# Sharing a TensorE transpose between the 64 tail columns of two x row tiles, in the head of a two-layer squared-ReLU kernel

## The chip, the cores and the metric

The kernel runs on one core of one Trainium2 chip. The metric is the device time of one execution in microseconds (us). The profile's *span* is measured from the first instruction to the last and is some 1.7 to 1.9 us shorter than the device time. Engines are named as the profile names them: PE is TensorE's matmuls, PEld its weight loads, DVE is VectorE, ACT is ScalarE, POOL is GpSimd, and SPq and ACTq are the queues on which DMA transfers are issued.

## The reference

```python
B, S, D, F = 1, 2048, 576, 4608            # all arrays bf16
h = einsum("bsd,df->bsf", x, w1) + b1
r = where(h > 0, h, 0)
out = einsum("bsf,fd->bsd", r * r, w2) + b2
```

The contraction length D = 576 is four and a half times the 128 rows of TensorE. The kernel cuts D into nine chunks of 64 columns, and most of the first layer runs as pairs of 64-row matmuls, one on each half of the array. Both halves need x transposed, with D on the partitions, and each half needs chunks that the other half holds. That is what the copies below are for.

## The kernel before

For the first block of 512 rows, x is loaded as four row tiles of 128 rows and transposed on TensorE. Four transposes of 128 columns cover columns 0 to 511. The last 64 columns need a fifth, which takes the last 128 columns, half of them for the second time.

```python
load_x(nc.sync, 0); load_x(nc.scalar, 1); load_x(nc.sync, 2); load_x(nc.scalar, 3)
for k in range(NK):                                  # NK = 4: chunks of w1n, 128 KB each
    load_w1n(nc.sync if k % 2 == 0 else nc.scalar, k, k + 1)
# ... cut ...
PLACE = [(0, 0), (0, 1), (1, 0), (1, 1), (0, 2)]
T_ORDER = [0, 1, NK, 2, 3]

def x_transpose(j):                                  # five transposes of one row tile
    h, q = divmod(j, 2)
    for k in T_ORDER:
        bank, slot = PLACE[k]
        c0 = k * P if k < NK else D - P
        transpose(tb[h][bank][:, slot, q*P:(q+1)*P], xs[:, j, c0:c0+P], ident)

def x_copies(h):                                     # PSUM -> xT0, for 256 rows
    for k in (0, 1): vector.tensor_copy(xT0[:, O+k, hc], tb[h][0][:, k, :])
    scalar.copy(xT0[:, O+2:O+4, hc], tb[h][1][:, 0:2, :])
    vector.tensor_copy(xT0[:, E3, hc], tb[h][0][:, 2, :])

def dup_windows(sb):                                 # shifted copies between the two halves
    vector.tensor_copy(xT[0:H, SPC:SPC+4, :], xT[H:P, E3:E3+4, :])
    vector.tensor_copy(xT[H:P, SPC:SPC+4, :], xT[0:H, O:O+4, :])

# the head ("keep" pins the order of the program):
for j in range(2): x_transpose(j)
x_copies(0)
for j in range(2, 4): x_transpose(j)
x_copies(1); dup_windows(0)
for k in range(NK): part(0, k)      # 4 matmuls of width 256 each: w1n chunk k, row half 0
part(1, 0); make_b1T()
for k in range(1, NK): part(1, k)
# then the row pair (w1n8, 64-row matmuls), their evictions, and the main loop over w1_h
```

Of the kernel before, what the change touches and what calls it, by code (L numbers as in the profile page):

```python
# [11 lines left out]
BF16 = mybir.dt.bfloat16  # L12
# [5 lines left out]
def kernel(  # L18
# [9 lines left out]
    nc = tc.nc  # L28
    keep = tc.keep_in_program_order
    P = 128  # L30
    H = 64
    x2 = x.flatten_outer_dims()
    out2 = out.flatten_outer_dims()
    S, D = x2.shape
# [3 lines left out]
    NK = NC // 2  # L38
# [6 lines left out]
    RT = SB // P  # L45
# [3 lines left out]
    const = ctx.enter_context(tc.tile_pool(name="const", bufs=1))  # L49
# [6 lines left out]
    ps_h = ctx.enter_context(tc.tile_pool(name="ps_h", bufs=4, space=PSUM))  # L56
# [8 lines left out]
    xs = const.tile([P, RT, D], BF16, name="x_sb")  # L65
# [12 lines left out]
    def load_w1n8(eng, h):  # L78
        keep(eng.dma_start(out=w1n8[h * H:(h + 1) * H, :], in_=w1[NK * P:D, 0:GW]))
# [14 lines left out]
    ident = const.tile([P, P], BF16, name="ident")  # L94
# [3 lines left out]
    keep(nc.scalar.dma_start(out=b1_rows[0:NFT, :], in_=b1.rearrange("(ft p) -> ft p", p=P)))  # L98
    for h in range(2):
        load_w1n8(nc.sync, h)  # L100

    E3, O, SPC, E = 0, 1, 5, 6
    LO_W = [O, O + 1, O + 2, O + 3, E, E + 1, E + 2, E3, SPC]
# [9 lines left out]
    def dup_windows(sb):  # L113
        xT = xT_blk[sb]
        keep(nc.vector.tensor_copy(out=xT[0:H, SPC:SPC + 4, :], in_=xT[H:P, E3:E3 + 4, :]))  # L115
        keep(nc.vector.tensor_copy(out=xT[H:P, SPC:SPC + 4, :], in_=xT[0:H, O:O + 4, :]))  # L116
# [18 lines left out]
    xT0 = xT_blk[0]  # L135
    HS = SB // 2
    tb = [[ps_h.tile([P, 4, HS], BF16, name="tb", tag="ph") for _ in range(2)] for _ in range(2)]
    PLACE = [(0, 0), (0, 1), (1, 0), (1, 1), (0, 2)]
    T_ORDER = [0, 1, NK, 2, 3]

    def x_transpose(j):
        h, q = divmod(j, 2)
        for k in T_ORDER:
            bank, slot = PLACE[k]
            c0 = k * P if k < NK else D - P
            keep(nc.tensor.transpose(tb[h][bank][:, slot, q * P:(q + 1) * P], xs[:, j, c0:c0 + P], ident[:]))

    def x_copies(h):
        hc = slice(h * HS, (h + 1) * HS)
        for k in (0, 1):  # L150
            keep(nc.vector.tensor_copy(out=xT0[:, O + k, hc], in_=tb[h][0][:, k, :]))
        keep(nc.scalar.copy(out=xT0[:, O + 2:O + 4, hc], in_=tb[h][1][:, 0:2, :]))  # L152
        keep(nc.vector.tensor_copy(out=xT0[:, E3, hc], in_=tb[h][0][:, 2, :]))

    b1T = const.tile([P, NFT], FP32, name="b1T")

    def make_b1T():
        b1T_ps = ps_h.tile([P, P], BF16, name="b1T_ps", tag="ph")
        keep(nc.tensor.transpose(b1T_ps[:], b1_rows[:], ident[:]))  # L159
        keep(nc.vector.tensor_copy(out=b1T[:], in_=b1T_ps[:, 0:NFT]))  # L160
# [6 lines left out]
    def evac_h(sb, bank, ft):  # L167
        r = rpool.tile([P, SB], BF16, name="r", tag="r")
        keep(nc.scalar.activation(out=r[:], in_=bank[:], func=ACT.Relu, bias=b1T[:, ft:ft + 1], scale=1.0))  # L169
        keep(nc.vector.tensor_tensor(out=hTs[sb][:, ft, :], in0=r[:], in1=r[:], op=ALU.mult))  # L170
# [17 lines left out]
    def a_full(sb, order):  # L188
        xT = xT_blk[sb]
        banks = []  # L190
        for g in range(G):
            pool, tag = (ps_o, "po") if g < 2 or order == "k_outer" else (ps_h, "ph")
            banks.append(pool.tile([P, SB], FP32, name="pn", tag=tag))

        def pair(i, start, stop):
            keep(nc.tensor.matmul(banks[2 * i][:], lhsT=w1n8[0:H, 2 * i * P:(2 * i + 1) * P], rhs=xT[0:H, SPC, :],  # L196
                             start=start, stop=stop, skip_group_check=order == "k_outer"))
            keep(nc.tensor.matmul(banks[2 * i + 1][:], lhsT=w1n8[H:P, (2 * i + 1) * P:(2 * i + 2) * P], rhs=xT[H:P, E3, :],  # L198
                             start=start, stop=stop, skip_group_check=order == "k_outer"))

        def full(g, k, start, stop):
            keep(nc.tensor.matmul(banks[g][:], lhsT=w1n[:, k, g * P:(g + 1) * P], rhs=xT[:, O + k, :],  # L202
                             start=start, stop=stop))

        if order == "rows_first":
            for i in (1, 0):
                pair(i, True, False)
            for g in (2, 3, 0, 1):
                for k in range(NK):
                    full(g, k, False, k == NK - 1)  # L210
                evac_h(sb, banks[g], g)
        else:
            if order == "k_outer":
                def part(h, k):
                    hc = slice(h * HS, (h + 1) * HS)
                    for g in range(G):
                        keep(nc.tensor.matmul(banks[g][:, hc], lhsT=w1n[:, k, g * P:(g + 1) * P],  # L217
                                              rhs=xT[:, O + k, hc], start=(h == 0 and k == 0), stop=False,
                                              skip_group_check=True))

                for j in range(2):
                    x_transpose(j)
                x_copies(0)
                for j in range(2, RT):
                    x_transpose(j)
                x_copies(1)
                dup_windows(0)
                for k in range(NK):
                    part(0, k)
                part(1, 0)  # L230
                make_b1T()
                for k in range(1, NK):
                    part(1, k)
            else:
                for g in (2, 3, 0, 1):
                    for k in range(NK):
                        full(g, k, k == 0, False)
            for i in (1, 0):
                pair(i, False, True)
                evac_h(sb, banks[2 * i], 2 * i)  # L240
                evac_h(sb, banks[2 * i + 1], 2 * i + 1)
# [42 lines left out]
    b2_col = const.tile([P, 1], BF16, name="b2_col")  # L284
    keep(nc.sync.dma_start(out=b2_col[:], in_=b2[DM:D].rearrange("(d o) -> d o", o=1)))
    b2T = const.tile([P, 1], FP32, name="b2T")
    nc.gpsimd.tensor_copy(out=b2T[:], in_=b2_col[:])
    keep(nc.sync.dma_start(out=b2_bc[:], in_=b2.partition_broadcast(P)))
    for c in range(2):
        load_w2(c)  # L290
# [1 line left out]

    alloc_hT(0)
    a_full(0, "k_outer")
    a_rows(0, 12, 1)
    alloc_hT(1)
    load_xT(3)
    a_rows(1)
    a_full(1, "rows_first")
    phase_t(0, hTs[0])  # L300
    phase_t(1, hTs[1])
    phase_b(0, hTs[0], dups=(2, 3))
    phase_b(1, hTs[1])
    alloc_hT(2)
    a_full(2, "g_outer")
    a_rows(2)
    alloc_hT(3)
# [36 lines left out]
```

## Time and profile before

| | before |
|---|---|
| device time, median | 290.67 us (three runs), 290.95 us with three more of the comparison |
| profiled span | 288.7 us |
| TensorE busy | 284.6 us, 99% of the span |
| first transposes / first chunk matmul / row pair / main loop | 3.76 / 5.41 / 9.06 / 9.50 us |

Everything that the change touches lies ahead of 9.5 us, and behind it TensorE runs without a break. The prediction shows TensorE's own lines of this stretch. What VectorE does in it, in order of time, is this (start, busy length, engine, line, operation, shapes, count, and the idle time before with its releaser):

```profile
4.42 0.49 DVE L151 COPY xTw<-tb 128x256 bf16<-128x256 bf16 x2 [3.49 <-PE tb L146]
6.44 0.69 DVE L115 COPY xTw<-xTw 64x2048 bf16<-64x2048 bf16 x1 [0.54 <-ACT xTw L152]
7.16 0.69 DVE L116 COPY xTw<-xTw 64x2048 bf16<-64x2048 bf16 x1
7.88 0.20 DVE L160 CAST b1T<-b1T_ps 128x36 f32<-128x36 bf16 x1
```

The shifted copies and the bias are finished at 8.08, and the row pair needs the copies at 9.06: VectorE is not late.

### The profile page before, as it was taken

To read this page: it belongs to the slowest core of one execution; us is meant where nothing else is said; L and a number is where in the kernel's file an instruction comes from. 1 tells how busy PE (TensorE), PEld (TensorE's weight loads), DVE (VectorE), ACT (ScalarE), POOL (GpSimd) and SP (SyncE) were. 2 spreads that over 40 slices of the span, in tenths; PEclk is the share of its full clock that TensorE was granted. 3 is DMA by queue.
4 is the path that set the end of the run, shared out by engine and by line. 5 is a ranking of instruction groups with operands and counts; after the bars stand their busy time and mean duration, and the time that the engine had idled before them with its cause. 6 is when DMAs were issued, how large, how long until landed. Compare 5 with 4: busy or idle time off the path is not lost.

```text
span 288.7 us, 4690 instructions
## 1 busy us (share of the span) xinstructions
PE 284.6 (99%) x2027; PEld 138.9 (48%) x2032; DVE 78.6 (27%) x177; ACT 96.5 (33%) x152; POOL 0.9 (0%) x7
## 2 busy tenths in 40 slices
PE   8999999999999999999999999999999999999996
PEld 5544444444444555555544444444444455555555
DVE  3444544444500200000025444444440001100001
ACT  3666666666500000000027666666670000000000
POOL 0000000000000000000000000000000000000000
PEclk9999999999999999999999999999999999999999
DMA  6999999600001100000000000000000110000000
GB/s 198 236 244 197 265 388 246 94 0 2 0 18 36 37 16 18 16 16 18 16 16 2 1 2 0 2 0 2 0 2 0 36 39 16 16 16 19 32 17 18
DMA packets 31573, 16.59 MB, mean 57 GB/s; under 512 B 15552, under 2 KB 31552, under 8 KB 31552
## 3 DMA queue, kind: packets, MB, share of 16 engines
q1 hardware_dynamic: 30928, 15.72, 22.3%
q10 hardware_dynamic: 624, 0.57, 0.7%
q8 instruction: 16, 0.26, 0.4%
q14 instruction: 5, 0.04, 0.0%
HBM read 11.43 MB, written 2.36 MB: 48 GB/s over the span
## 4 chain that ended last, share of the span: by engine, by line
PE 97%; DMA 1%; SPq 0%; issue 0%; DVE 0%
PE ph L181 42%; PE po L272 38%; PE pt L253 11%; PE pn L202 4%; DMA w1n<-in_w_dram 1%; PE pn L217 1%; PE ph L183 1%; PE pn L196 1%; SPq L72 0%; DVE o_sb L274 0%; PE b1T_ps L159 0%; PE pn L198 0%
## 5 line engine op out<-in xcount | busy, mean ns | idle before, releaser
L181 PE MATMUL ph<-xTw,w_h 64*128 64x512 bf16 x576 | 124.6, 376 | 0.0
L183 PE MATMUL ph<-xTw,w_h 64*128 64x512 bf16 x576 | 124.6, 376 | 0.0
L272 PE MATMUL po<-w_sb,hT 128*128 128x448 bf16 (+2 forms) x612 | 109.4, 341 | 0.0
L169 ACT ACTIVATE r<-ph,b1T 128x512 bf16<-128x512 f32 x128 | 81.1, 685 | 41.6 <-PE ph L183 41.6
L181 PEld LDWEIGHTS <-w_h 64*128 64x128 bf16 x576 | 54.1, 94 | 68.3
L272 PEld LDWEIGHTS <-hT 128*128 128x128 bf16 x612 | 58.5, 98 | 51.0
L170 DVE TENSOR_TENSOR hT<-r 128x512 bf16<-128x512 bf16 x144 | 61.2, 426 | 76.9 <-ACT r L169 76.9
L183 PEld LDWEIGHTS <-w_h 64*128 64x128 bf16 x576 | 54.1, 94 | 0.0
L274 DVE TENSOR_TENSOR o_sb<-po,b_bc 128x448 bf16<-128x448 f32 (+2 forms) x17 | 10.2, 597 | 125.8 <-PE po L272 125.8
L253 PE MATMUL pt<-hT,w_sb 128*128 128x512 bf16 x142 | 31.3, 379 | 0.1
L169 ACT ACTIVATE r<-pn,b1T 128x512 bf16<-128x512 f32 x16 | 10.3, 688 | 62.0 <-PE pn L198 60.6
L253 PEld LDWEIGHTS <-w_sb 128*128 128x128 bf16 x144 | 14.1, 98 | 17.0
L256 ACT ACTIVATE oT<-pt,b2T 128x512 bf16<-128x512 f32 x4 | 2.7, 687 | 28.3 <-PE pt L253 28.3
L202 PE MATMUL pn<-xTw,w1n 128*128 128x512 bf16 x45 | 10.4, 379 | 0.4 <-issue 0.3
L202 PEld LDWEIGHTS <-w1n 128*128 128x128 bf16 x48 | 4.5, 98 | 6.0 <-issue 0.8
L217 PE MATMUL pn<-xTw,w1n 128*128 128x256 bf16 x32 | 3.7, 273 | 0.1
L63 PE MATMUL wps<-const-bfloat16-1.0 128*128 128x512 bf16 (+1 forms) x7 | 2.9, 597 | 0.8 <-PEq L328 0.8
L217 PEld LDWEIGHTS <-w1n 128*128 128x128 bf16 x32 | 3.0, 98 | 0.6 <-DMA w1n<-in_w_dram 0.3
L115 DVE COPY xTw<-xTw 64x2048 bf16<-64x2048 bf16 x4 | 2.8, 690 | 0.6 <-ACT xTw L152 0.5
L116 DVE COPY xTw<-xTw 64x2048 bf16<-64x2048 bf16 x4 | 2.8, 688 | 0.1
L196 PE MATMUL pn<-xTw,w1n 64*128 64x512 bf16 x8 | 2.4, 379 | 0.0
L198 PE MATMUL pn<-xTw,w1n 64*128 64x512 bf16 x8 | 2.4, 379 | 0.0
(21 smaller groups left out, 10.5 us busy)
## 6 DMA issues: line engine op xcount, KB each, us to landing
w_sb<-in_w_dram SPq DMA_DIRECT2D x2, 2592.0 KB, 15.2
w_h<-in_w_dram SPq DMA_DIRECT2D x14, 288.0 KB, 6.6
out_dram<-o_sb SPq DMA_DIRECT2D x15, 112.0 KB, 1.7
w_h<-in_w_dram SPq DMA_DIRECT2D x4, 144.0 KB, 3.2
out_dram<-ot SPq DMA_DIRECT2D x4, 128.0 KB, 2.0
x_sb<-in_x_dram ACTq DMA_DIRECT2D x2, 144.0 KB, 3.0
x_sb<-in_x_dram SPq DMA_DIRECT2D x2, 144.0 KB, 3.0
w1n<-in_w_dram ACTq DMA_DIRECT2D x2, 128.0 KB, 3.6
```

The lines of the kernel that those rows point to most:

```text
L63: keep(nc.tensor.matmul(wps[:, 0:n], lhsT=ones[:, 0:P], rhs=ones[:, 0:n], start=True, stop=True))
L115: keep(nc.vector.tensor_copy(out=xT[0:H, SPC:SPC + 4, :], in_=xT[H:P, E3:E3 + 4, :]))
L169: keep(nc.scalar.activation(out=r[:], in_=bank[:], func=ACT.Relu, bias=b1T[:, ft:ft + 1], scale=1.0))
L170: keep(nc.vector.tensor_tensor(out=hTs[sb][:, ft, :], in0=r[:], in1=r[:], op=ALU.mult))
L181: keep(nc.tensor.matmul(bx[:], lhsT=w1_h[0:H, LO_C[i], jc], rhs=xT[0:H, LO_W[i], :], start=(i == 0), stop=(i == NC - 1)))
L183: keep(nc.tensor.matmul(by[:], lhsT=w1_h[H:P, UP_C[i], jc], rhs=xT[H:P, UP_W[i], :], start=(i == 0), stop=(i == NC - 1)))
L196: keep(nc.tensor.matmul(banks[2 * i][:], lhsT=w1n8[0:H, 2 * i * P:(2 * i + 1) * P], rhs=xT[0:H, SPC, :], start=start, stop=stop, skip_grou ...
L202: keep(nc.tensor.matmul(banks[g][:], lhsT=w1n[:, k, g * P:(g + 1) * P], rhs=xT[:, O + k, :], start=start, stop=stop))
L217: keep(nc.tensor.matmul(banks[g][:, hc], lhsT=w1n[:, k, g * P:(g + 1) * P], rhs=xT[:, O + k, hc], start=(h == 0 and k == 0), stop=False, s ...
L253: keep(nc.tensor.matmul(pt[:], lhsT=w2_sb[:, ft, DM:D], rhs=hT[:, ft, :], start=(i == 0), stop=(i == NFT - 1)))
L272: keep(nc.tensor.matmul(po[:, 0:d1 - d0], lhsT=hT[:, ft, jj * P:(jj + 1) * P], rhs=w2_sb[:, ft, d0:d1], start=(i == 0), stop=(i == NFT - 1)))
L274: keep(nc.vector.tensor_tensor(out=o_sb[:, d0:d1], in0=po[:, 0:d1 - d0], in1=b2_bc[:, d0:d1], op=ALU.add))
```

## The change

The intent is a shorter head. Each row tile gets four transposes instead of five. The 64 tail columns of two row tiles are first put side by side by GpSimd (`xs8`), so that one transpose serves both, and these two transposes stand behind chunk 1 of the first half instead of ahead of all matmuls. The copies from PSUM are ordered bank by bank, with VectorE taking the first half alone. One of the shifted copies of block 0 goes to ScalarE.

```diff
+    xs8 = const.tile([P, RT, H], BF16, name="xs8")
+    for h in range(2):
+        keep(nc.gpsimd.tensor_copy(out=xs8[:, 2 * h:2 * h + 2, :], in_=xs[:, 2 * h:2 * h + 2, NK * P:D]))
...
     def x_transpose(j):
-        for k in T_ORDER:                      # five, see above
+        for bank in range(2):
+            for k in range(2 * bank, 2 * bank + 2):
+                transpose(tb[h][bank][:, k % 2, q*P:(q+1)*P], xs[:, j, k*P:(k+1)*P], ident)
+            for k in range(2 * bank, 2 * bank + 2) if q == 1 else ():
+                copy = nc.scalar.copy if h == 1 and bank == 1 else nc.vector.tensor_copy
+                copy(xT0[:, O + k, hc], tb[h][bank][:, k % 2, :])
+    def dup_windows_first():
+        scalar.copy(xT0[0:H, E:E + 3, :], xT0[H:P, O:O + 3, :])
+    def transpose_tails():
+        for h in range(2):
+            transpose(tl[:, h, :], xs8[:, 2*h:2*h+2, :], ident)
+        for q in range(2): vector.tensor_copy(x8[H:P, E3, :, q, :], tl[q*H:(q+1)*H, 0:2, :])
+        for q in range(2): vector.tensor_copy(x8[0:H, SPC, :, q, :], tl[q*H:(q+1)*H, 0:2, :])
+        vector.tensor_copy(xT0[H:P, SPC:SPC + 4, :], xT0[0:H, O:O + 4, :])
+        vector.tensor_copy(xT0[0:H, E3, :], xT0[H:P, O + 3, :])
...
-                (transposes, x_copies, dup_windows(0), part(0, 0..3), part(1, 0), make_b1T, part(1, 1..3))
+                for j in range(RT): x_transpose(j)
+                dup_windows_first()
+                part(0, 0); part(0, 1)
+                transpose_tails()
+                part(0, 2); part(0, 3)
+                for k in range(NK):
+                    part(1, k)
+                    if k == 1: make_b1T()
```

(Wrappers are dropped from some lines. One tiny copy of `b2` is also pinned in the program order.)

More of the change, by code (lines that the diff above doesn't have):

```diff
@@ L137 @@
     tb = [[ps_h.tile([P, 4, HS], BF16, name="tb", tag="ph") for _ in range(2)] for _ in range(2)]
-    PLACE = [(0, 0), (0, 1), (1, 0), (1, 1), (0, 2)]
-    T_ORDER = [0, 1, NK, 2, 3]
     def x_transpose(j):
         h, q = divmod(j, 2)
-        for k in T_ORDER:
-            bank, slot = PLACE[k]
-            c0 = k * P if k < NK else D - P
-            keep(nc.tensor.transpose(tb[h][bank][:, slot, q * P:(q + 1) * P], xs[:, j, c0:c0 + P], ident[:]))
-    def x_copies(h):
-        hc = slice(h * HS, (h + 1) * HS)
-        for k in (0, 1):
-            keep(nc.vector.tensor_copy(out=xT0[:, O + k, hc], in_=tb[h][0][:, k, :]))
-        keep(nc.scalar.copy(out=xT0[:, O + 2:O + 4, hc], in_=tb[h][1][:, 0:2, :]))
-        keep(nc.vector.tensor_copy(out=xT0[:, E3, hc], in_=tb[h][0][:, 2, :]))
-    b1T = const.tile([P, NFT], FP32, name="b1T")
+        hc = slice(h * HS, (h + 1) * HS)
+        for bank in range(2):
+            for k in range(2 * bank, 2 * bank + 2):
+                keep(nc.tensor.transpose(tb[h][bank][:, k % 2, q * P:(q + 1) * P], xs[:, j, k * P:(k + 1) * P], ident[:]))
+            for k in range(2 * bank, 2 * bank + 2) if q == 1 else ():
+                copy = nc.scalar.copy if h == 1 and bank == 1 else nc.vector.tensor_copy
+                keep(copy(out=xT0[:, O + k, hc], in_=tb[h][bank][:, k % 2, :]))
+    b1T = const.tile([P, NFT], FP32, name="b1T")
+    def dup_windows_first():
+        keep(nc.scalar.copy(out=xT0[0:H, E:E + 3, :], in_=xT0[H:P, O:O + 3, :]))
+    def transpose_tails():
+        tl = ps_h.tile([P, 2, P], BF16, name="tl", tag="ph")
+        for h in range(2):
+            keep(nc.tensor.transpose(tl[:, h, :], xs8[:, 2 * h:2 * h + 2, :], ident[:]))
+        x8 = xT0.rearrange("p c (h q t) -> p c h q t", h=2, q=2)
+        for q in range(2):
+            keep(nc.vector.tensor_copy(out=x8[H:P, E3, :, q, :], in_=tl[q * H:(q + 1) * H, 0:2, :]))
+        for q in range(2):
+            keep(nc.vector.tensor_copy(out=x8[0:H, SPC, :, q, :], in_=tl[q * H:(q + 1) * H, 0:2, :]))
+        keep(nc.vector.tensor_copy(out=xT0[H:P, SPC:SPC + 4, :], in_=xT0[0:H, O:O + 4, :]))
+        keep(nc.vector.tensor_copy(out=xT0[0:H, E3, :], in_=xT0[H:P, O + 3, :]))
     def make_b1T():
@@ L219, in part @@
                                               skip_group_check=True))
-                for j in range(2):
+                for j in range(RT):
                     x_transpose(j)
-                x_copies(0)
-                for j in range(2, RT):
-                    x_transpose(j)
-                x_copies(1)
-                dup_windows(0)
+                dup_windows_first()
+                part(0, 0)
+                part(0, 1)
+                transpose_tails()
+                part(0, 2)
+                part(0, 3)
                 for k in range(NK):
-                    part(0, k)
-                part(1, 0)
-                make_b1T()
-                for k in range(1, NK):
                     part(1, k)
+                    if k == 1:
+                        make_b1T()
             else:
@@ L286 @@
     b2T = const.tile([P, 1], FP32, name="b2T")
-    nc.gpsimd.tensor_copy(out=b2T[:], in_=b2_col[:])
+    keep(nc.gpsimd.tensor_copy(out=b2T[:], in_=b2_col[:]))
     keep(nc.sync.dma_start(out=b2_bc[:], in_=b2.partition_broadcast(P)))
```

## The prediction

> **What bounds the kernel now.** I read the page first (busy shares, then the chain of waits that ended last), then the chain over the first 10 us, and then the timeline of that stretch engine by engine, because the diff touches nothing that runs after about 10 us except one tiny GpSimd copy.
>
> ```profile
> PE 284.6 (99%) x2027; PEld 138.9 (48%) x2032; DVE 78.6 (27%) x177; ACT 96.5 (33%) x152; POOL 0.9 (0%) x7
> PE 97%; DMA 1%; SPq 0%; issue 0%; DVE 0%
> ```
>
> The first line gives busy time per engine in a span of 288.7 us; the second is the share of the chain that ended last. TensorE holds 97% of that chain. So only two things can change the time: the moment at which TensorE starts on work that it then never leaves, and the number of instructions it executes after that moment. The chain over the first 10 us (start, length, what) shows where that moment is:
>
> ```profile
> 0.73 0.40 SPq L72
> 1.20 0.44 SPq L72
> 1.68 3.68 DMA w1n<-in_w_dram
> 5.36 0.05 issue
> 5.41 2.36 PE pn L217 x20
> 7.76 0.06 PE b1T_ps L159
> 7.82 1.31 PE pn L217 x12
> 9.13 0.32 PE pn L196
> ```
>
> The reader is to see that no transpose of x is in it. The path goes through two issues of x loads on the SyncE queue, the load of the first chunk of w1n (3.68 us, landing at 5.36), and then TensorE from 5.41 without a hole: 20 matmuls of L217, the bias transpose, 12 more, the row pair of L196 and L198, and the main loop. Before 5.41 TensorE waits three times, and the timeline of its weight loads says for what:
>
> ```profile
> 3.76 0.56 PEld L146 LDWEIGHTS <-x_sb 128*128 128x128 bf16 x10 [0.75 <-DMA x_sb<-in_x_dram]
> 4.55 0.56 PEld L146 LDWEIGHTS <-x_sb 128*128 128x128 bf16 x10 [0.23 <-DMA x_sb<-in_x_dram]
> 5.40 2.08 PEld L217 LDWEIGHTS <-w1n 128*128 128x128 bf16 x20 [0.29 <-DMA w1n<-in_w_dram]
> ```
>
> Columns are start, busy length, engine, line, instruction, count, and in brackets the idle time before it with its releaser. All 20 transposes of the kernel before lie between 3.76 and 5.11, in two lots of ten, each lot behind an x load; afterwards TensorE idles 0.29 us for w1n. The transposes have slack of 0.29 us.
>
> **What the Trainium skill says.** (1) "TensorE: Matmul & The Clock Gate", Back-to-back issue gap, gives 134 cycles for a moving width of 128 and 262 for 256, which at its 2.4 GHz are 56 ns and 109 ns. The trace agrees: 20 matmuls of width 256 with a duration of 0.273 us took 2.36 us, so their spacing is (2.36 - 0.27)/19 = 0.110 us, and ten transposes kept the weight load busy 0.56 us, 0.056 us each. (2) "VectorE: DVE Perf Modes", perf-mode tier table: a bf16 copy of 2048 elements from SBUF takes 693 ns in the 4x mode, anything from PSUM is capped at 2x. The window copies of L115 and L116 measure 690 ns, so they agree; the copies from PSUM take 0.286 us for 256 elements, two of them in 0.49 us, so one each 0.20 us. (3) "GPSIMD Engine Reference", 3.1, puts elementwise work at 1.8 cycles per element at best; at its 1.2 GHz that is an estimate of 0.19 us for 128 elements. The trace has a GpSimd operation on 128x128 (the second step of the identity) at 0.294 us, and I use 0.3 us. (4) "Advanced Engine Details and Errata", Mode Summary, says that VectorE's second SBUF port is shared with GpSimd, and that they block each other. No row of the kernel before shows such a collision, as GpSimd has nothing to do after 1.3 us there.
>
> **The change part by part.**
>
> *Removed on TensorE:* each of four row tiles had five transposes, one of which (the last 128 columns) was mostly columns already transposed. Now there are four per tile: 20 becomes 16, less 4 x 0.056 = 0.22 us. All four were in front of 5.41, beside a load. The second lot would end about 2 x 0.056 = 0.11 us sooner, at about 5.00, and TensorE would then wait some 0.40 us instead of 0.29 for the same w1n chunk. Gain on the path: nothing, as long as w1n is last.
>
> *Added on TensorE:* two transposes of the tails, between chunks 1 and 2 of the first half. That is after 5.41, on the path: + 2 x 0.056 = +0.11 us. The bias transpose moves from after 20 matmuls to after 24, but costs its 0.06 us in both. The matmuls themselves, 32 of width 256, the pairs and everything later are the same in count and order.
>
> *Copies per bank:* the order is changed so that the first half's chunks 2 and 3 are copied by VectorE instead of ScalarE. Six VectorE copies at 0.20 us pitch, four of them from about 4.45 and two behind the last tile at about 5.0, should be done at about 5.7. The second matmul chunk of the first half starts at 5.41 + 4 x 0.11 = 5.85, chunk 2 at 5.41 + 8 x 0.11 + 0.11 = 6.40: ample. ScalarE has two copies of 256 elements instead of two of 512 (0.588 us each); it can start at 5.33, when it ends issuing the bias load, as before, and is done near 6.0.
>
> *The tail's GpSimd copies:* two copies of 128x128 at 0.3 us, the second when x tiles 2 and 3 are there (4.5). Done at about 5.1 by this estimate; the first tail transpose is issued at 5.41 + 8 x 0.11 = 6.29. Slack about 1.2 us.
>
> *Window copies:* before, two VectorE copies of 0.69 us ended at 7.85. Now ScalarE does the first, 64x1536. The two ScalarE durations in the trace, 0.20 us for one element (L97) and 0.588 us for 512, give a slope of 0.76 ns per element, so by estimate 0.20 + 1536 x 0.00076 = 1.37 us, from 6.0 to 7.4. VectorE waits for the tails (in PSUM at about 6.35 + 0.22 = 6.57), makes four copies of them (7.5), then the 2048-element copy (8.2), a 512-element copy of an estimated 0.3 us (8.5) and the bias cast of 0.20 us (8.7).
>
> *Who needs them:* the row pair, at 9.06 + 0.11 = 9.17, reads what the tail copies wrote (7.5; slack 1.6). The main loop reads the shifted copies from its fifth pair on, at about 9.6 + 4 x 0.216 = 10.5 (VectorE 8.5, ScalarE 7.4). The first eviction, at 9.48 + 0.11, needs the bias (8.7; slack 0.9). The order of waits in the built kernel agrees: nothing new stands in front of the first L217 matmul, and the waits for the shifted copies stand inside the main loop.
>
> *Sum:* 5.41 unchanged, +0.11 for the two tail transposes, 0 elsewhere: +0.11 us, 290.67 + 0.11 = 290.78 us. It is a change meant to shorten the head that, in this trace, takes from a stretch with slack and adds to one without.
>
> **The rivals.**
>
> *A. The w1n load is not really last.* If without the profiler, or in most executions, w1n lands before 5.1, transposes are what TensorE waits for, and the net count (20 to 18) counts: -2 x 0.056 = -0.11 us, 290.56. Against it: the trace shows 0.29 us of waiting behind the transposes. For it: the three timings spread over 0.68 us and I have one trace.
>
> *B. A tail wait takes the place of the transposes.* GpSimd may be held off by VectorE's port use or be slow on a 64-wide strided pattern. It has 1.2 us of slack; if each copy took 1.2 us instead of 0.3, TensorE would stall about 0.6 us and the time would be 291.4. For it: two engines hand over in a row (GpSimd, TensorE, VectorE), and no copy of this kind is in the trace. Against it: the 0.294 us row, and VectorE's copies at that time come from PSUM, for which the skill's tier table excludes the two-port modes.
>
> *C. VectorE's queue becomes the bound of the head.* It ends at 8.7 instead of 8.08 (the bias cast at 7.88 + 0.20); if the tails come late by over 0.9 us, the first eviction waits for the bias, and after two more banks TensorE waits too. That needs B first.
>
> *D. Earlier matmuls run into later weight loads.* Only if the head got shorter: the main loop's first weight loads take 3.2 us from their issues at 4.8, so they land at about 8.0, before 9.5. Not a threat at +0.11.
>
> **Range and chances.** The middle is between the sum (290.78, about two in three) and A (290.56), with B at one in ten: 290.75. The three timings of the kernel before reach from 290.65 to 291.33, so a median could stand 0.3 lower or 0.5 higher without any cause in the kernel: 290.4 to 291.3. Two per cent would be 5.8 us, more than the whole stretch between the first transposes and the main loop (9.5 - 3.8 = 5.7); nothing here can move that much, so within 2% gets 0.98.
>
> **What would show it right or wrong.** In the profile after: 16 transposes ahead of the first w1n matmul, that matmul still at 5.4 behind a DMA wait of w1n grown to about 0.4 us; two tail transposes near 6.3 with no idle before them; the row pair at about 9.17 and the main loop at about 9.6, both 0.11 later than before; span about 288.8. A main loop that starts at 9.4 or sooner says A. An idle gap in front of the tail transposes with GpSimd as releaser says B. A gap in front of the first eviction released by VectorE says C. The prediction is wrong if w1n lands at another time than 5.36, since that one load sets the start of all that follows, or if a matmul, after the bank layout or order changed, runs at another spacing than before.

## More of the kernel before

The seven warm-up matmuls at the very start (`wps`) work on constants. They exist only to have TensorE running before the first data lands.

## The result, and the profile after

The changed kernel took **291.02 us** (median of six runs, 290.69 to 291.51), beside **290.95 us** for the kernel before (six runs, 290.65 to 291.33). The ratio is 1.0003, with a 95% interval of 0.999 to 1.0016: the same. A ratio is the mean time of one kernel's runs over that of the other's of the same rounds, so it is not quite the ratio of these medians. The middle of the prediction was 290.75 us, and the measured time lies within its range of 290.4 to 291.3.

TensorE's weight loads in the head of the changed kernel, to be read beside the three lines in the prediction:

```profile
3.42 1.63 PEld L147 LDWEIGHTS <-x_sb 128*128 128x128 bf16 x16 [0.41 <-DMA x_sb<-in_x_dram]
5.30 0.77 PEld L229 LDWEIGHTS <-w1n 128*128 128x128 bf16 x8 [0.24 <-DMA w1n<-in_w_dram]
6.08 0.21 PEld L160 LDWEIGHTS <-xs 128*128 128x128 bf16 x2
6.24 1.68 PEld L229 LDWEIGHTS <-w1n 128*128 128x128 bf16 x16
```

Two things are as forecast. The first chunk matmul still stands behind a wait for w1n, and the two tail transposes (L160) have no idle time before them, so they lie on the path. One thing is not. Sixteen weight loads of transposes keep the engine busy for 1.63 us, where twenty took 0.56 + 0.56 us before. The chain of waits (start, length, what) shows the same:

```profile
0.78 2.93 PE wps L63 x7
3.71 0.65 PE tb L147 x6
4.38 0.89 DVE xTw L150 x4
5.30 1.05 PE pn L229 x8
6.35 0.11 PE tl L160 x2
6.46 1.75 PE pn L229 x16
8.21 0.06 PE b1T_ps L171
8.26 0.87 PE pn L229 x8
9.13 0.32 PE pn L208
```

Six transposes in 0.65 us are 0.108 us each, twice the 0.056 us of the kernel before. In this execution the changed kernel made all but the last two or three of its transposes at half speed. The two tail transposes cost 0.11 us (6.35 to 6.46), as predicted.

The third line is a trap. It suggests that VectorE's four copies released the first chunk matmul. But that matmul reads only what the first copy wrote, which took 0.28 us from 4.38 and so was done at 4.66. (In e10 below, where this code is the same, the first chunk matmul starts at 4.64 while the four copies last from 4.29 to 5.18.) The fourth copy merely ended at 5.27, beside the landing of w1n. The releaser in the weight loads' view, w1n, is the right one. A chain is inferred, and two events 0.03 us apart can change places in it.

The other engines in the same stretch:

```profile
4.38 1.28 DVE L150 COPY xTw<-tb 128x256 bf16<-128x256 bf16 x6 [3.45 <-PE tb L147]
6.50 0.59 DVE L163 COPY xTw<-tl 64x256 bf16<-64x256 bf16 x2 [0.83 <-PE tl L160]
7.10 0.59 DVE L165 COPY xTw<-tl 64x256 bf16<-64x256 bf16 x2
7.72 0.69 DVE L166 COPY xTw<-xTw 64x2048 bf16<-64x2048 bf16 x1
8.76 0.20 DVE L172 CAST b1T<-b1T_ps 128x36 f32<-128x36 bf16 x1
5.93 1.47 ACT L155 COPY xTw<-xTw 64x1536 bf16<-64x1536 bf16 x1
4.34 0.29 POOL L103 COPY xs<-x_sb 128x128 bf16<-128x128 bf16 x1 [0.45 <-DMA x_sb<-in_x_dram]
```

The shifted copies and the bias are now done at 8.96 instead of 8.08, still ahead of the row pair at 9.07 and the first eviction at 9.49. GpSimd is done at 4.63, and the first tail transpose comes at 6.18.

### The profile page after: what moved, and what is told of

Same layout as the page of the kernel before. It is cut to its first block, busy times and chain, and to the rows that moved or that the text cites. A ratio compares the mean times of both kernels' runs of the same rounds, so it can differ in the third digit from the quotient of the medians.

```text
span 288.8 us, 4702 instructions
## 1 busy us (share of the span) xinstructions
PE 285.3 (99%) x2030; PEld 143.1 (50%) x2030; DVE 79.1 (27%) x181; ACT 97.4 (34%) x153; POOL 1.5 (1%) x9
## 3 DMA queue, kind: packets, MB, share of 16 engines
HBM read 11.43 MB, written 2.36 MB: 48 GB/s over the span
## 4 chain that ended last, share of the span: by engine, by line
PE 98%; DVE 0%; issue 0%
PE ph L193 41%; PE po L283 38%; PE pt L264 11%; PE pn L214 4%; PE ph L195 2%; PE pn L229 1%; PE wps L63 1%; PE pn L208 1%; DVE xTw L150 0%; PE tb L147 0%; DVE o_sb L285 0%; PE tl L160 0%; PE b1T_ps L171 0%; PE pn L210 0%
## 5 line engine op out<-in xcount | busy, mean ns | idle before, releaser
L150 DVE COPY xTw<-tb 128x256 bf16<-128x256 bf16 x6 | 1.3, 281 | 3.5 <-PE tb L147 3.5
```

## The experiments

**What was to be told apart.** The theory after reading both traces: the landing of w1n sets the start of the chunk matmuls; the transposes ahead of it have slack, so removing some is worth nothing; the two tail transposes behind it cost their own 0.11 us. On top of that lie things that vary from execution to execution and that both kernels share, among them the speed of the transposes. (The expectations call the cause of that speed the clock gate; it is explained under e1.) The rivals: the half-speed transposes belong to the changed kernel; the transposes are what the start waits for; the GpSimd copies or VectorE's queue are near the path.

The table collects the moments from every trace (us). The record lists e1 to e4 on one chip, e5 to e8 on a second and e9 to e12 on a third; within the first alone the first chunk matmul lies between 5.26 and 5.76, so that spread is not one between chips. "w1n wait" is the idle time of the weight loads ahead of the first chunk matmul that is put down to w1n. A kernel's row pair comes after its chunk matmuls.

| trace | first chunk matmul | w1n wait | row pair | between them | span | span minus row pair |
|---|---|---|---|---|---|---|
| before | 5.41 | 0.29 | 9.06 | 3.65 | 288.7 | 279.6 |
| before, again (e1) | 5.76 | 0.18 | 9.77 | 4.01 | 289.5 | 279.7 |
| after | 5.30 | 0.24 | 9.07 | 3.77 | 288.8 | 279.7 |
| after, again (e2) | 5.51 | 0.28 | 9.52 | 4.01 | 289.2 | 279.7 |
| tails early (e3) | 5.58 | 0.52 | 9.24 | 3.66 | 288.9 | 279.7 |
| 16 behind (e4) | 5.26 | none | 9.93 | 4.67 | 289.6 | 279.7 |
| 16 ahead (e5) | 5.99 | none | 9.75 | 3.76 | 290.6 | 280.9 |
| 16 ahead, again (e11) | 6.40 | none | 10.15 | 3.75 | 289.8 | 279.7 |
| GpSimd x4 (e8) | 5.51 | 0.60 | 9.28 | 3.77 | 289.0 | 279.7 |
| copy on VectorE (e12) | 5.63 | 0.45 | 9.47 | 3.84 | 289.4 | 279.9 |
| before, no warm-up (e6) | 5.76 | none | 10.45 | 4.69 | 290.1 | 279.7 |
| after, no warm-up (e7) | 5.76 | 0.70 | 11.03 | 5.27 | 290.7 | 279.7 |
| w1n early (e9) | 4.86 | none | 9.87 | 5.01 | 289.8 | 279.9 |
| w1n early, w_h x2 (e10) | 4.64 | none | 9.11 | 4.47 | 289.7 | 280.6 |

The last column is the most useful. Unless TensorE waits for `w_h` later on, the span is the moment of the row pair plus 279.7 us, whatever was done to the head. (It did wait in e5, e9, e10 and e12.) So a trace says where in the head a time came from, where timings of one kernel spread over 0.8 us. The column "between them" may be compared to a few hundredths of a microsecond, but only among traces whose chunk matmuls all ran at full speed. In e1, e2, e6, e7 and e9 the first of them ran at half speed, some 0.107 us more for each, which is why e1 and e2 both show 4.01. In e12 the second chunk of w1n came late and added a wait of 0.06.

### e1 and e2: both kernels once more, unchanged

> The kernel before, unchanged, looked at once more. Theory (w1n sets the start of the chunk matmuls, and the transposes ahead of it run at full or at half speed as the clock gate's phase falls): the transposes' spacing in this look is 0.056 us, 0.107 us or a mix. At 0.056 the first chunk matmul stands at 5.3 to 5.4 behind a wait for w1n; at 0.107 twenty transposes take 2.1 us and end at 5.6 or later, and the first chunk matmul follows them with no w1n wait. Rival (the gate's phase is the same in every execution, and the slow transposes belong to the changed kernel): 0.056 us and 5.3 to 5.4 again.

> The changed kernel, unchanged. Theory: time ratio to before 0.998 to 1.002; the two tail transposes cost 0.11 us behind the start in any look. The transposes' spacing may differ from the 0.107 us of the first look. Rival (the slow transposes are a property of the changed kernel): spacing 0.107 us again, first chunk matmul within 0.1 us after the last transpose.

The kernel before, in its second look:

```profile
3.29 2.28 PEld L146 LDWEIGHTS <-x_sb 128*128 128x128 bf16 x20 [0.28 <-DMA x_sb<-in_x_dram]
5.75 2.44 PEld L217 LDWEIGHTS <-w1n 128*128 128x128 bf16 x20 [0.18 <-DMA w1n<-in_w_dram]
3.71 2.13 PE tb L146 x20
```

(The third line is of the chain of waits.) Twenty transposes took 2.13 us, 0.107 us each: half speed also befalls the kernel before. The first twenty chunk matmuls were partly slow too (2.72 us instead of 2.36), and this execution took 291.23 us. The changed kernel's second look was slow again (16 in 1.79 us) and its five timings gave a median of 291.14 us, ratio 1.0007 (0.9994 to 1.002). That look alone would fit the rival. e1 above refutes it, and so do e3 and e4 below, two variants of the changed kernel: their second eight transposes kept the weight loads busy for 0.45 us, 0.056 us each.

"TensorE: Matmul & The Clock Gate" in the Trainium skill (Part 1) describes this: TensorE's clock is gated to half until a free-running window of some 3.4 us has seen it busy, so that the moment of opening varies from run to run. The traces agree. The spacing is 0.107 or 0.056 us, nothing else for long, while PEclk in the profile stays at 1.00, so the halving doesn't show there. In the first look of the kernel before the gate was open at the first transpose (3.76). By estimate from e1's extra 0.36 us, at an extra 0.107 us for each slow matmul, it opened there after some 3.4 chunk matmuls, near 6.5.

In e1 the twenty transposes just fitted although the gate was closed: its weight loads ended at 3.29 + 2.28 = 5.57 and the wait for w1n ended at 5.75. That wait's end itself moved between the looks, from 5.30 to 5.75. With a closed gate and an earlier w1n, the old kernel's transposes are the later ones, and the change gains there. e6 below shows this without warm-up: w1n landed at about 5.5 (issued at 1.66, 3.8 us to landing), and the first chunk matmul came at 5.76, behind the transposes. By estimate e2 was such an execution too. There w1n let the chunk matmuls start at 5.51, while twenty transposes at 0.107 us from 3.50 last until 5.64, so the kernel before would have lost some 0.13 us, about as much as the two tail transposes cost. So "worth nothing" holds where a wait for w1n is left, and not in every execution.

### e3: the tail transposes ahead of the first chunk matmul

```diff
+                transpose_tails()
                 part(0, 0)
                 part(0, 1)
-                transpose_tails()
```

> Changed kernel with the two tail transposes put ahead of the first chunk matmul. Theory: from the first chunk matmul to the row pair takes 0.11 us less than in the changed kernel (3.77 us there, from 5.30 to 9.07), so 3.66; the first chunk matmul itself stays on w1n's landing as long as the transposes end before it. Time 0 to 0.11 us less than the changed kernel, under what the timings resolve. Rival (tails are free where they stand, hidden under weight loads): 3.77 us stays.

The stretch is 3.66 us, the forecast to the hundredth. The transposes now stand in the slack: TensorE's weight loads still wait for w1n behind them.

```profile
4.87 0.19 PEld L160 LDWEIGHTS <-xs 128*128 128x128 bf16 x2
5.58 2.52 PEld L229 LDWEIGHTS <-w1n 128*128 128x128 bf16 x24 [0.52 <-DMA w1n<-in_w_dram]
```

The timings (290.85 to 291.04, median 290.93, ratio to before 1.0002) cannot resolve 0.11 us, as expected.

### e4, e5 and e11: sixteen more transposes, behind or ahead of the first chunk matmul

```diff
 # e4, in transpose_tails, tl made larger; the results are not used
+        for e in range(16):
+            transpose(tl[:, 2 + e % 6, :], xs[:, e % RT, 0:P], ident)
 # e5 and e11, at the top of x_transpose(3), into unused slots of tb
+        for e in range(16): transpose(tb[1][e % 2][:, 2 + e//2 % 2, ...], xs[:, j, 0:P], ident)
```

> Changed kernel with 16 more transposes (results unused) right behind the two tail ones. Theory: these lie on the path, 16 x 0.056 = +0.90 us in time and in the stretch from first chunk matmul to row pair (3.77 to 4.67). Rival (work there hides in slack): less than +0.3 us.

The stretch is 4.67 us, again as forecast: 0.90 us more than the 3.77 of the changed kernel.

```profile
6.04 0.21 PEld L160 LDWEIGHTS <-xs 128*128 128x128 bf16 x2
6.21 0.94 PEld L162 LDWEIGHTS <-x_sb 128*128 128x128 bf16 x16
7.10 1.68 PEld L231 LDWEIGHTS <-w1n 128*128 128x128 bf16 x16
```

The mean of its four timings, 291.93 us, is 0.85 above that of the changed kernel in the same rounds (291.08). Behind the start, a transpose costs its full 0.056 us.

> Changed kernel with 16 more transposes (results unused) ahead of the fourth x tile's own, that is ahead of the first chunk matmul. Theory: the wait for w1n absorbs the first 0.3 to 0.4 us of them if the clock gate is open: 16 x 0.056 - 0.35 = +0.55 us; if they run at half speed, up to 16 x 0.107 = +1.7 us; no w1n wait is left before the first chunk matmul. Rival (transposes are always what the first chunk matmul waits for): at least +0.90 us at full speed, with no slack eaten.

No w1n wait was left, as expected, and the first chunk matmul came at 5.99. The chunk of w1n that it reads was issued at 1.66 and took 4.1 us, so it landed at about 5.7 and would have allowed a start at about 5.75. So the sixteen transposes, though twelve of the others ran at half speed, delayed the start by some 0.2 us and not by their 0.90; the forecast had been 0.55. But the four timings were 291.45 to 292.97, ratio 1.0046 (1.0021 to 1.0071), and the trace shows why: a wait of 0.82 us of TensorE for `w_h` at 15.28. That was not foreseen, and it called for a repeat. The chain that ends at this wait holds no transpose:

```profile
1.67 4.27 DMA w1n<-in_w_dram
5.95 0.61 SPq L82
8.65 6.58 DMA w_h<-in_w_dram
```

(Three `w_h` issues between the last two lines are left out. The w1n load of this chain is the one for chunk 1, issued on ACTq, and not the one that the first chunk matmul reads.) By this chain the wait came from late loads, and not from the padding.

> The kernel with 16 more transposes ahead of the first chunk matmul, once more: its first look had a wait of 0.82 us for w_h near 15 us, which no other look had. Theory (w_h's landing varies from run to run, and the padding does not cause it): no such wait in this look, and single times between 291.4 and 291.9, with 293 only where the gate opens late. Rival (the padding delays the loads): a wait for w_h of 0.5 us or more again.

There was no wait for `w_h` this time; the four timings were 291.62 to 292.18, the highest above the forecast of 291.9, and the ratio 1.0027 (1.0014 to 1.0041), some 0.8 us over the kernel before (0.0027 x 291). Here part of the transposes ran at half speed (32 from 3.52 to about 6.35, so 0.088 us each on average). The w1n chunk landed at about 5.4 (issued at 1.66, 3.7 us), and the first chunk matmul came at 6.40, so here the padding delayed the start by some 0.9 us. By the timings alone, ahead (e11) and behind (e4) are hardly told apart. It is the trace of e5 that shows the slack, and how much of it there is depends on the execution.

### e6 and e7: without warm-up

```diff
-    WARM = [512] * 6 + [256]
+    WARM = [512]
```

> Kernel before with one warm-up matmul instead of seven, so that the clock gate is closed during all transposes. Theory: 20 transposes at 0.107 us from about 3.6 end at about 5.8, the first chunk matmul stands at about 5.8 with no w1n wait ahead of it; the chunk matmuls too run at half speed, so the time is 2 to 4 us longer than with the warm-up. Rival (w1n is last whatever the clock): first chunk matmul at 5.3 to 5.4.

> Changed kernel with one warm-up matmul instead of seven. Theory: 16 transposes at 0.107 us end at about 5.4, the first chunk matmul stands at 5.3 to 5.45, some 0.4 us before that of the kernel before without warm-up; the tails cost 2 x 0.107 = 0.21 us; so main loop some 0.2 us earlier than in the kernel before without warm-up, if the gate opens at the same moment. Rival: no difference in the start, main loop 0.2 us later.

In e6 the first chunk matmul stood at 5.76 behind twenty slow transposes with no w1n wait, as expected: here the transposes, and not w1n, set the start. Its time was only 0.9 us longer than the kernel before with warm-up (291.8 against 290.88), not 2 to 4. In e7 it also stood at 5.76, but for another reason: w1n landed only at 5.72 in that execution, and the weight loads waited 0.70 us for it. So the expected lead of 0.4 us was not seen. e7 was slower than e6 (292.43 against 291.8) and the traces show the gate opening by estimate near 8.9 instead of 7.9, from the counts of slow matmuls. The pair compares two gate phases and is **inconclusive** on the change.

### e8: each GpSimd copy made four times

> Changed kernel with each of the two GpSimd copies of the tails made four times. At 0.29 us each the eight take 2.4 us from 3.6, or 4 x 0.29 behind the last x tile: done at about 6.0. Theory (over 1 us of slack before the first tail transpose at 6.18): no idle gap ahead of the tail transposes over 0.1 us, time within 0.2 us of the changed kernel. Rival (the GpSimd copy is near the path): an idle gap of about 1 us ahead of the tail transposes, +1 us.

```profile
3.70 2.64 POOL L103 COPY xs<-x_sb 128x128 bf16<-128x128 bf16 x8 [2.39 <-DMA x_sb<-in_x_dram]
6.29 0.21 PEld L160 LDWEIGHTS <-xs 128*128 128x128 bf16 x2
```

GpSimd was busy until 6.34 (expected: about 6.0), and the tail transposes (6.40) had no gap before them. The stretch stayed at 3.77 and the ratio was 1.0003. The GpSimd copies have slack of more than a microsecond.

### e12: the shifted copy back on VectorE

```diff
-        keep(nc.scalar.copy(out=xT0[0:H, E:E + 3, :], in_=xT0[H:P, O:O + 3, :]))
+        keep(nc.vector.tensor_copy(out=xT0[0:H, E:E + 3, :], in_=xT0[H:P, O:O + 3, :]))
```

> Changed kernel with the shifted copy 64x1536 put back on VectorE. Theory (VectorE has slack in the head, so that moving this copy to ScalarE is worth nothing): the copy takes about 0.5 us (2048 elements take 0.69) and fills the gap of 0.83 us that VectorE has ahead of the tail copies in the changed kernel; the bias is ready by 9.3 at a row pair near 9.1 to 9.5, the first eviction is not delayed, time within 0.2 us of the changed kernel. Rival (VectorE's queue is the bound of the head without the move): the first eviction waits for VectorE, +0.3 us or more.

```profile
5.89 0.56 DVE L155 COPY xTw<-xTw 64x1536 bf16<-64x1536 bf16 x1
6.90 0.59 DVE L163 COPY xTw<-tl 64x256 bf16<-64x256 bf16 x2 [0.45 <-PE tl L160]
9.16 0.20 DVE L172 CAST b1T<-b1T_ps 128x36 f32<-128x36 bf16 x1
```

The copy takes 0.56 us on VectorE where ScalarE needs 1.47, and it falls into the gap that VectorE has there anyway. The bias was ready at 9.36 and the first eviction started at 9.89. A wait of 0.40 us for `w_h` at 14.07, not foreseen, is in this trace too. The ratio to before is 1.0004 (0.999 to 1.0018). The part of the change that uses ScalarE is worth nothing either way.

### e9 and e10: load w1n earlier, to beat both

If w1n sets the start, its loads should go ahead of those of x tiles 2 and 3.

```diff
-    load_x(nc.sync, 0); load_x(nc.scalar, 1); load_x(nc.sync, 2); load_x(nc.scalar, 3)
-    for k in range(NK): load_w1n(...)
+    for q in range(2):
+        load_x(nc.sync, 2*q); load_x(nc.scalar, 2*q+1)
+        load_w1n(nc.sync, 2*q, 2*q+1); load_w1n(nc.scalar, 2*q+1, 2*q+2)
...
+    order: transposes of tiles 0, 1; part(0, 0), part(0, 1); transposes of 2, 3; part(0, 2); tails; part(0, 3); ...
 # e10 besides:
-    for (j0, j1) in [(0, 1), (1, 2), (2, 4), ...
+    for (j0, j1) in [(0, 2), (2, 4), ...
```

> Changed kernel with the loads of w1n chunks 0 and 1 put ahead of those of x tiles 2 and 3, and in TensorE's order chunks 0 and 1 of the first half ahead of the transposes of those tiles. Theory (the landing of w1n sets the start of the chunk matmuls): first chunk matmul at 4.6 to 4.9 instead of 5.3 to 5.8, row pair at 8.7 to 9.1 instead of 9.07 to 9.5. But the third row group's weights (the second load of w_h for row groups 2 and 3) landed at about 13.0 in the kernel before, only 0.4 us ahead of their use, so part of this comes back as a wait of TensorE for w_h near 13 us: time 0.2 to 0.5 us less than before. Rival (w1n is not the gate; the copies are): first chunk matmul stays at 5.3 or later.

> As the run with early w1n loads, and the first w_h loads made two row groups wide instead of one, two issues fewer on the SyncE queue. Theory: the loads for row groups 2 and 3 are issued 1.3 us sooner, so no wait for w_h near 13 us is left; the first pair lands near 9.2, when the main loop starts, so a wait of 0 to 0.4 us may stand there instead. Time 0.4 to 0.8 us less than the kernel before. Rival (w_h is bound by its bytes, not by its issues): a wait for w_h of the same size, at the first row group or the third.

The first half of the theory held: the first chunk matmul moved to 4.86 and 4.64. But neither is faster: e9 has a median of 291.43 us, ratio 1.0006 (0.999 to 1.0022), and e10 291.85 us, ratio 1.0027 (1.0014 to 1.0039). The weight loads of e10 say what took the gain:

```profile
6.22 0.33 PEld L228 LDWEIGHTS <-w1n 128*128 128x128 bf16 x4 [0.27 <-DMA w1n<-in_w_dram]
10.28 0.09 PEld L194 LDWEIGHTS <-w_h 64*128 64x128 bf16 x1 [0.84 <-DMA w_h<-in_w_dram]
```

What was loaded later is waited for later: chunk 2 of w1n at 6.22 (in e9 at 6.97), and then the main loop's weights. Besides, the eight transposes of tiles 2 and 3 now stand behind the start, where they cost 0.45 us in e10. These 0.45 and the wait of 0.27 account for the 0.70 us by which its stretch exceeds the 3.77 of the changed kernel, so its row pair, at 9.11, is no earlier. In e9 a closed gate adds to it: the first eight chunk matmuls took 1.61 us, against 1.03 in e10, and the row pair came at 9.87 instead of the expected 8.7 to 9.1. With w1n early, the first chunk matmul waits for VectorE's first copy (an idle time of 0.27 us in e10). In e9 the wait for `w_h`, expected near 13, came as 0.33 us at 14.41; in e10 the first row group's load, made twice as wide, landed at 10.24 instead of the expected 9.2. In these two runs, moving one load forward only moved the waits to the loads behind it. No version beat the kernel before.

## Why the prediction was right or wrong

- **"The transposes have slack", gain on the path nothing**: right in kind for the traces at hand. A wait for w1n was left ahead of the first chunk matmul in both looks of both kernels (0.18 to 0.29 us). But with a closed gate the removed transposes can be worth some 0.1 us (the estimate from e2 above), which the prediction has only under another cause, rival A. The wait's size was taken from one execution: the w1n wait was to grow to about 0.40 and was 0.24 and 0.28.
- **The two tail transposes, +0.11 us**: right, and the best measured number here. With the gate open the stretch from first chunk matmul to row pair went from 3.65 to 3.77, came back to 3.66 when they were moved ahead (e3), and rose by 0.90 when sixteen more were put beside them (e4).
- **"5.41 unchanged"**: right on average, wrong as a constant. The landing of w1n, and with it or the transposes the first chunk matmul, lay between 5.26 and 5.76 in looks at the two kernels and at variants that left their loads alone and kept the warm-up (e3, e4, e8, e12). In the first look after it was 5.30, 0.11 us early, which hid the 0.11 us of the tails exactly: the main loop started at 9.51 after and 9.50 before, and not at the predicted 9.6.
- **The 0.056 us for every transpose** is the step that failed. It held for the two tail transposes in every trace with warm-up in which they stand behind the start; ahead of the start the spacing was 0.056 or 0.107 us, from one execution to the next. The prediction named "another spacing than before" as what would make it wrong, but as an effect of the banks. That the weight loads of the transposes ended at 3.42 + 1.63 = 5.05, near the predicted 5.00, was luck: they took 1.63 us but began 0.34 us earlier than in the kernel before.
- **The side engines**: GpSimd at 0.3 us was right (0.29). ScalarE's shifted copy took 1.47 us against 1.37. The four tail copies on VectorE took 1.2 us against the 0.9 of the estimate, since they come 0.30 us apart and not 0.20. Their inputs alternate between partition 0 and partition 64, and "VectorE: DVE Perf Modes" (Two Vector instructions with no wait between them) says, as a model, that an instruction whose input starts in another quadrant (group of 32 partitions) than the one before is held until all earlier ones have finished; a spacing of 0.30 us at a duration of 0.29 agrees. The bias came at 8.96 instead of 8.7. None of it was on the path.
- **Rival A** (w1n not last) is real in single executions: in e4 no w1n wait was left, because x tiles 2 and 3 came late (TensorE began its last eight transposes at 4.76), in e6 the transposes came last, and in e1 the wait was 0.18 us. **Rival B** fell with e8. **Rival C** fell with the first trace (bias at 8.96, first eviction at 9.49), and e12 found no bound on VectorE either. **Rival D** was dismissed too early. It looked only at the first loads of `w_h`; those for the third row group land about 0.4 us before use, and e9 and e10 ran into such loads. Even without a shorter head, e12 had a wait of 0.40 us at 14.07 and e5 the one at 15.28. In e5, e9 and e12 SyncE's second issue for `w_h` started at 5.95, 5.96 and 6.11, against 5.49 in the kernel before; why it was held is not shown.
- **The time**: the sum said +0.11 us and the blend of rivals +0.08; the medians differ by 0.07 and the ratio by 0.0003, both far inside the noise. That the two tail transposes cost 0.11 us is shown by the traces' stretch, not by the times; the sign of the whole change over many executions is not shown.

## What to carry to other kernels

Before removing work, find the wait behind it: work ahead of a wait has a price only beyond that wait, while work put behind it is paid in full, so a reordering that reduces the count can still add time. In a head that waits for data, take more than one trace before trusting a spacing or a landing as a constant. When one load is moved forward, look at the next loads whose slack is smaller than the gain.

## What the Trainium skill lacked or had wrong

- "TensorE: Matmul & The Clock Gate", Part 4, says that the full clock doesn't engage for transposes, which don't count as busy in the same way as matmuls. The first half did not hold here: with the gate open transposes came 0.056 us apart, and in e4 the gate opened in the middle of eight of them (0.77 us of weight loads, against 0.45 for the next eight). Whether transposes count as busy stays open. In e6 the gate opened (an estimate from the count of slow matmuls) near 7.9, 2.1 us after the first chunk matmul and 4.2 after the first transpose; but in the first look of the kernel before it was open at 3.76, 2.98 us after the first warm-up matmul and before any transpose. No run isolates it.
- The same part gives 275 ns for a 128x128 bf16 transpose in a kernel; here one lasted 219 ns with the gate open and about 311 ns with it closed, and what counts on the path is the spacing of 56 or 107 ns.
- "GPSIMD Engine Reference", 3.1, has rates per element and no time for a small copy: 128x128 bf16 took 0.29 us, and eight of them in a row 2.64 us.
- No page that was read has the spread of a load's landing at the start of a program: the same 128 KB of w1n, issued at about 1.7, landed between about 5.25 and 5.7 in four looks at the same two kernels, more than the whole effect under study.
